# One ring of four PSUM banks for attention's transposes, products and mixing outputs, in place of two rings of two

## The chip, the cores and the metric

The kernel runs on one core of a Trainium2 chip. The metric is the device time of one execution in microseconds (us), lower is better; three runs of the kernel before gave 731.08, 732.12 and 732.07 us, median 732.07. The engines are named as the profile names them: PE is TensorE's matmul (PEld its weight load), DVE is VectorE, ACT is ScalarE, POOL is GpSimd, SP is SyncE, which issues the loads.

## What is computed

Causal attention over 2 batches, 12 heads, 448 positions and 64 channels per head, then two layers on the (2, 448, 768) result, all in float32:

```python
def _attn_ref(q, k, v):
    scores = scale * np.matmul(q, k.transpose(0, 1, 3, 2))
    scores = np.where(mask, -1000000000.0, scores)
    scores = scores - np.max(scores, axis=-1, keepdims=True)
    attn = np.exp(scores)
    attn = attn / (np.sum(attn, axis=-1, keepdims=True) + 1e-09)
    return np.matmul(attn, v).astype(np.float32)

def _moe_ref(x, w_tok1, w_tok2, w_ch1, w_ch2):
    xt = x.transpose(0, 2, 1)
    h = np.maximum(xt @ w_tok1, 0.0) @ w_tok2
    u = x + h.transpose(0, 2, 1)
    h2 = np.maximum(u @ w_ch1, 0.0) @ w_ch2
    return (u + h2).astype(np.float32)

def _moe2_ref(x, w_ch1, w_ch2):
    mixed = np.real(np.fft.fft(np.fft.fft(x, axis=1), axis=2)).astype(np.float32)
    u = x + mixed
    un = (u - mu) / np.sqrt(var + 1e-06)
    ch = np.maximum(un @ w_ch1, 0.0) @ w_ch2
    return (u + ch).astype(np.float32)
```

The weights of the MLPs arrive as float64.

## The kernel before

**Stages.** Attention with token mixing takes the first 170 us or so; the first channel MLP, the Fourier transform and the second channel MLP follow. Products of full precision are made of three passes over operands split in a high and a low part (kh and kl, qh and ql, wh and wl). Weights are fetched as 64-bit words (`fetch`, L73) and turned into such parts by `convert_steps` (L76 to L101): two instructions on ScalarE (L82, L99), four on VectorE (L84, L85, L89, L93), one on GpSimd (L100). Some of these conversions are put between the steps of attention by `weights` (L415).

**One pair of heads.** Attention goes through 12 pairs of heads. `prep` loads k and q and splits them (L196 to L206). `scores(n, g)` makes the scores of pair n in three groups g of row blocks: matmuls (L230, L243) into a tile b_s, row maxima on VectorE (L247), exponentials on ScalarE (L256) into the tile p in SBUF. `transposes(n, u)` for u = 0 to 4 turns four 112x112 blocks of p each into a PSUM tile (L269), which is copied to the tile pt, by ScalarE for u = 1 and 3 (L274), by VectorE for u = 0, 2 and 4 (L276). `pv` multiplies pt with v (L284) and ScalarE copies the result to ots (L289). `finish` transposes the head outputs back (L305), and VectorE scales them with the row sums into x (L307), splits them (L313), GpSimd makes the low part (L314).

**Token mixing.** After every third pair half a batch is complete. `mix_in` (L330, evicted by L336 on ScalarE and L337 on VectorE) and `channels_first` (L342, evicted by L345 on ScalarE) run in the steps `mix_first` and `mix_second`; three steps `mix_out` (L364, evicted by L366 on VectorE) follow. `next_mix` puts two such steps into each iteration.

**The order of the work.** TensorE's order is written out by hand (L424 on); the loop's n, by which the stages are named here, runs from 0 to 13. An iteration issues, in this order: scores(n, 0), pv of pair n - 2, scores(n, 1), transposes u = 0 and 1 of pair n - 1, a mixing step, transposes u = 2, scores(n, 2), transposes u = 3 and 4, a mixing step, finish of pair n - 2. The order on the other engines is the scheduler's, which also decides which free bank a new tile takes; every engine then works its queue off in order.

**PSUM.** It has eight banks, all used here: b_s has two buffers of two banks; tiles b_t (`transposes`, `channels_first`) share two banks; tiles b_y (`ybank`: pv, `finish`, `mix_in`, `mix_out`, and the last group of scores of the very first pair) share two others. The lines that say so:

```python
        ps = actx.enter_context(tc.tile_pool(name="aps", bufs=2, space=bass.MemoryType.PSUM))

        def ybank():
            return ps.tile([128, 512], F32, tag="y", name="b_y")
...
            tv = ps.tile([128, 512], F32, tag="t", name="b_t", bufs=2)
```

A tile that takes a bank waits until the bank's last content has been copied out. `spread` (L714), in the second MLP, has two small tiles r and nt.

Of the kernel before, what the change touches and what calls it, by code (L numbers as in the profile page):

```python
# [10 lines left out]
F32 = mybir.dt.float32  # L11
# [10 lines left out]
TS = 112  # L22
NI = S // TS
# [19 lines left out]
def fused_kernel(ctx: ExitStack, tc: tile.TileContext, qk, v, w1, w2, wa, wb, wc, wd, fa, fa0, fb, out):  # L43
# [107 lines left out]
    with ExitStack() as actx:  # L151
        ps = actx.enter_context(tc.tile_pool(name="aps", bufs=2, space=bass.MemoryType.PSUM))

        def ybank():
            return ps.tile([128, 512], F32, tag="y", name="b_y")

        ap = actx.enter_context(tc.tile_pool(name="attn", bufs=2))
        a1 = actx.enter_context(tc.tile_pool(name="attn1", bufs=1))
# [53 lines left out]
        def scores(n, g):  # L212
# [5 lines left out]
            if n or g < 2:  # L218
                sp = ps.tile([128, 2, 512], F32, tag="s", name="b_s", bufs=2)
                se = [sp[:TS, e] for e in range(2)]  # L220
            else:
                se = [ybank()[:TS] for e in range(2)]
# [38 lines left out]
        def transposes(n, u):  # L261
            c = pairs[n]
            if u == 0:
                c.pt = ap.tile([TS, 5, S], F32, tag="pt", name="pt", bufs=1)
            tv = ps.tile([128, 512], F32, tag="t", name="b_t", bufs=2)
            col = 0
            for e, j in (((0, 0),), ((1, 0),), ((0, 1), (0, 3)), ((1, 1), (1, 3)), ((0, 2), (1, 2)))[u]:
                for i in range(j, NI):
                    nc.tensor.transpose(  # L269
                        tv[:TS, col : col + TS], c.p[:, e, OFF[i] + j * TS : OFF[i] + (j + 1) * TS], ident[:TS, :TS]  # L270
                    )
                    col += TS
            if u in (1, 3):
                mark[1] = act.copy(c.pt[:, u], tv[:TS, :S]).ins  # L274
            else:
                mark[0] = vec.tensor_copy(c.pt[:, u], tv[:TS, :S]).ins  # L276

        def pv(n):
            c = pairs[n]
            c.ot = ybank()  # L280
            for j in range(NI):
                for e in range(2):
                    u, col = ((e, 0), (2 + e, 0), (4, 224 * e), (2 + e, 336))[j]
                    mm(  # L284
                        c.ot[D * e : D * e + D, j * TS : S], lhsT=c.v[:, j, D * e : D * e + D],
                        rhs=c.pt[:, u, col : col + TS * (NI - j)], start=j == 0, stop=j == NI - 1,
                    )
            c.ots = ap.tile([128, S], F32, tag="ots", name="ots")
            act.copy(c.ots, c.ot[:, :S])  # L289

        def finish(n):
            c = pairs[n]
            b, hf, pr = n // 6, n % 6 // 3, n % 3
            if pr == 0:
                h = Pair()
                halves[2 * b + hf] = h
                h.x = ap.tile([TS, NI, XW], F32, tag="x32", name="x32", bufs=1)
                h.h = ap.tile([TS, NI, XW], F32R, tag="xh", name="xh", bufs=1)
                h.l = ap.tile([TS, NI, XW], F32R, tag="xl", name="xl", bufs=1)
            h = halves[2 * b + hf]  # L300
            vec.tensor_scalar(out=c.ssum, in0=c.ssum, scalar1=1.0e-9, scalar2=None, op0=ALU.add)
            vec.reciprocal(out=c.ssum, in_=c.ssum)
            xp = ybank()
            for i in range(NI):
                nc.tensor.transpose(xp[:TS, i * 128 : (i + 1) * 128], c.ots[:, i * TS : (i + 1) * TS], ident)  # L305
            sl = slice(hf + pr * 128, hf + pr * 128 + 128)
            vec.tensor_tensor(  # L307
                out=h.x[:, :, sl].rearrange("p i (e d) -> p i e d", e=2),
                in0=xp[:TS, :].rearrange("p (i e d) -> p i e d", i=NI, e=2),
                in1=c.ssum.to_broadcast([TS, NI, 2, D]),  # L310
                op=ALU.mult,
            )
            vec.tensor_copy(h.h[:, :, sl], h.x[:, :, sl])  # L313
            pool.tensor_tensor(out=h.l[:, :, sl], in0=h.x[:, :, sl], in1=f(h.h)[:, :, sl], op=ALU.subtract)  # L314
            if hf and pr == 2:
                vec.tensor_copy(h.x[:, :, 0:1], h.x[:, :, 384:385])
                copied = vec.tensor_copy(h.h[:, :, 0:1], f(h.h)[:, :, 384:385])
                if n == 6 * B - 1:
                    hold.append(copied.ins)
                pool.tensor_copy(h.l[:, :, 0:1], f(h.l)[:, :, 384:385])  # L320
# [16 lines left out]
            vec.scalar_tensor_tensor(out=tl, in0=hp[:, :384], scalar=0.0, in1=f(th), op0=ALU.max, op1=ALU.subtract)  # L337

        def channels_first(n, pr):
            xt = ps.tile([128, 512], F32, tag="t", name="b_t", bufs=2)  # L340
            for i in range(NI):
                nc.tensor.transpose(  # L342
                    xt[:, i * TS : (i + 1) * TS], halves[n].x[:, i, pr * 128 : (pr + 1) * 128], ident[:TS, :TS]
                )
            act.copy(resid[3 * (n % 2) + pr][n // 2], xt[:, :S])  # L345

        def mix_first(n, t):
            mix_in(n, t)
            channels_first(n, 0)

        def mix_second(n, t):
            mix_in(n, t)
            channels_first(n, 1)
            channels_first(n, 2)
# [69 lines left out]
        with tc.manual_schedule(engines={mybir.EngineType.PE}):  # L424
            for n in range(np_ + 2):
# [15 lines left out]
                if old:  # L441
                    transposes(n - 1, 0)
                    transposes(n - 1, 1)
# [3 lines left out]
                if old:  # L447
                    transposes(n - 1, 2)
# [23 lines left out]
    ps = ctx.enter_context(tc.tile_pool(name="ps", bufs=1, space=bass.MemoryType.PSUM))  # L472
# [4 lines left out]
    def bank(tag=None):  # L477
        if tag is None:
            tag = cyc[turn[0] % 8]
            turn[0] += 1  # L480
        return ps.tile([128, 512], F32, tag=tag, name="b_" + tag, bufs=depth[tag])
# [232 lines left out]
    def spread(b, p):  # L714
        acc = rstd[b]
        var = bank()[:TS, :NI]
        with tc.issue_after(tail[0]):
            for i in range(NI):
                mm(var[:, i : i + 1], lhsT=acc[:, i * TS : (i + 1) * TS], rhs=mean_w[:, :1], start=True, stop=True)
        r = p.tile([TS, 16], F32, name=f"r{b}")[:, :NI]  # L720
        nt = p.tile([TS, 16], F32, tag="nt", name="nt")[:, :NI]
        act.activation(out=r, in_=var, func=AF.Sqrt, bias=eps_t[:TS], scale=1.0)
        vec.reciprocal(out=r, in_=r)
        vec.tensor_tensor(out=nt, in0=r, in1=r, op=ALU.mult)
        vec.scalar_tensor_tensor(out=nt, in0=var, scalar=EPS, in1=nt, op0=ALU.add, op1=ALU.mult)
        vec.tensor_scalar(out=nt, in0=nt, scalar1=-0.5, scalar2=1.5, op0=ALU.mult, op1=ALU.add)
        vec.tensor_tensor(out=r, in0=r, in1=nt, op=ALU.mult)
        inv[b] = r
# [34 lines left out]
    with tc.tile_pool(name="g2", bufs=1) as gpool, tc.tile_pool(name="tp", bufs=2) as tpool:  # L763
        wide_pool[0] = gpool
        late = {4: lambda: variance(0, gpool), 5: lambda: variance(1, gpool),
                6: lambda: spread(0, gpool), 7: lambda: spread(1, gpool)}
        for n in range(3):
            g = mlp_up(gpool, wc[n], 8, () if n else ahead, None if n else late)
            mlp_down(wd[n], g, scaled_store if n == 2 else scaled_add, 1)
# [73 lines left out]
```

## Time and profile before

| what | value |
|---|---|
| median of three runs | 732.07 us |
| the profiled execution's own time | 731.05 us |
| its span in the profile | 729.3 us |
| PE busy | 698.6 us, 96% of the span |
| PEld busy | 630.3 us, 86% |
| DVE busy | 523.6 us, 72% |
| ACT busy | 285.1 us, 39% |
| POOL busy | 275.3 us, 38% |
| chain of work that ended last | PE 77%, DVE 12%, ACT 5% of the span |

The profiled execution lies 1.0 us below the median. Busy shares are averages over stages with different limits. In a timeline the bracket at a line's end is the idle time of that engine just before the line, and what ended it; matmuls are pipelined, so that a line's duration reaches past the next line's start.

### The profile page before, as it was taken

Reading aid. Unit: us, or ns where it says so; the run is one execution under the profiler, and the core shown is the slowest. Engines: PE = TensorE matmul, PEld = TensorE weight load, DVE = VectorE, ACT = ScalarE, POOL = GpSimd, SP = SyncE. Lnnn points to the kernel's source line nnn. Section 1 sums busy time; section 2 is a strip of 40 time slices with the busy share of each in tenths; the row PEclk is TensorE's granted clock in tenths of the full one; section 3 lists DMA queues with packets and bytes.
Section 4 is the critical chain, followed back from the end, with each engine's and each line's share of the span. In section 5 each row is a group of like instructions: output and inputs, shape, how many; then the busy total and the mean of one; then the engine's idle time right before and its main releaser. Section 6 shows DMA issues by size and latency. Waiting matters only on the chain.

```text
span 729.3 us, 10268 instructions
## 1 busy us (share of the span) xinstructions
PE 698.6 (96%) x3940; PEld 630.3 (86%) x3940; DVE 523.6 (72%) x808; ACT 285.1 (39%) x600; POOL 275.3 (38%) x197
## 2 busy tenths in 40 slices
PE   6889899999999999999899999999999999999997
PEld 4668677878899999998689999999999999999996
DVE  5888887455698895688979997767945686945722
ACT  7777767334224333223353452223432222432200
POOL 3233634255133242241377334465323446321210
PEclk9989999999999999999999999999999999999999
DMA  8142411018533433210022242242321434322311
GB/s 265 54 127 88 140 35 56 30 32 263 138 137 118 148 125 115 87 44 0 1 86 87 88 146 102 100 173 90 131 97 58 145 106 155 114 89 83 113 50 51
DMA packets 20608, 74.15 MB, mean 102 GB/s; under 512 B 2364, under 2 KB 6974, under 8 KB 20192
## 3 DMA queue, kind: packets, MB, share of 16 engines
q1 hardware_dynamic: 19952, 69.48, 28.4%
q0 software_dynamic: 608, 4.03, 1.9%
q8 instruction: 31, 0.51, 0.3%
q14 instruction: 17, 0.14, 0.1%
HBM read 70.75 MB, written 2.75 MB: 101 GB/s over the span
## 4 chain that ended last, share of the span: by engine, by line
PE 77%; DVE 12%; ACT 5%; DMA 2%; POOL 2%; issue 2%; ACTq 0%; POOLq 0%; SPq 0%; DVEq 0%
PE b_s L144 6%; PE b_s L145 6%; PE b_s L143 6%; PE b_s L506 5%; PE b_s L507 5%; PE b_s L508 5%; PE b_t L508 3%; PE b_s L230 3%; PE b_t L506 3%; PE b_t L507 3%; PE b_t L143 2%; PE b_t L144 2%; PE b_t L145 2%; PE b_t L269 2%; ACT p L256 2%; PE b_y L284 2%
## 5 line engine op out<-in xcount | busy, mean ns | idle before, releaser
L100 POOL TENSOR_TENSOR wl<-m,wh 128x512 fp32r<-128x512 f32 (+1 forms) x90 | 149.4, 1660 | 253.6 <-ACT wh L99 240.9
L82 ACT ACTIVATE m<-w 128x512 f32<-128x512 f32 (+2 forms) x92 | 71.2, 773 | 165.9 <-POOL wl L100 131.7
L84 DVE TENSOR_SCALAR m<-m 128x512 f32<-128x512 f32 (+2 forms) x92 | 51.5, 560 | 88.8 <-ACT m L82 88.7
L89 DVE SCALAR_TENSOR_TENSOR m<-w,m 128x512 uint32<-128x512 uint32 (+2 forms) x92 | 101.2, 1101 | 2.4
L93 DVE SCALAR_TENSOR_TENSOR m<-w,m 128x512 uint32<-128x512 uint32 (+2 forms) x92 | 100.2, 1090 | 1.5
L99 ACT CAST wh<-m 128x512 fp32r<-128x512 f32 (+1 forms) x90 | 63.3, 703 | 94.3 <-DVE m L93 51.4
L143 PE MATMUL b_s<-acth,wh 128*128 128x448 f32 x240 | 87.2, 363 | 1.5 <-DVE resid L366 1.5
L144 PE MATMUL b_s<-acth,wl 128*128 128x448 f32 x240 | 86.9, 362 | 0.0
L145 PE MATMUL b_s<-actl,wh 128*128 128x448 f32 x240 | 86.6, 362 | 0.0
L506 PE MATMUL b_s<-gh,wh 128*128 128x448 f32 x208 | 75.7, 364 | 0.0
L508 PE MATMUL b_s<-gl,wh 128*128 128x448 f32 x208 | 75.3, 362 | 0.0
L507 PE MATMUL b_s<-gh,wl 128*128 128x448 f32 x208 | 75.2, 362 | 0.0
L256 ACT ACTIVATE p<-b_s,nmx 112x112 f32<-112x112 f32 (+3 forms) x94 | 45.3, 497 | 24.9 <-DVE nmx L247 20.6
L748 POOL TENSOR_TENSOR resid<-t,resid 128x448 f32<-128x448 f32 x24 | 33.7, 1402 | 49.5 <-DVE t L747 46.1
L85 DVE TENSOR_SCALAR m<-m 128x512 uint32<-128x512 uint32 (+2 forms) x92 | 49.6, 540 | 2.2
L143 PEld LDWEIGHTS b_s<-acth,wh 128*128 128x128 f32 x240 | 45.0, 187 | 4.8 <-issue 1.8
L145 PEld LDWEIGHTS b_s<-actl,wh 128*128 128x128 f32 x240 | 45.0, 187 | 3.1
L144 PEld LDWEIGHTS b_s<-acth,wl 128*128 128x128 f32 x240 | 45.0, 188 | 2.9
L508 PE MATMUL b_t<-gl,wh 128*128 128x448 f32 x120 | 43.6, 363 | 1.3 <-DVE gl L147 1.3
L506 PE MATMUL b_t<-gh,wh 128*128 128x448 f32 x120 | 43.7, 364 | 0.0
L507 PE MATMUL b_t<-gh,wl 128*128 128x448 f32 x120 | 43.4, 362 | 0.0
L269 PE MATMUL b_t<-ident,p 112*112 112x112 f32 x240 | 32.3, 274 | 11.5 <-DVE pt L276 6.4
(260 smaller groups left out, 1538.3 us busy)
## 6 DMA issues: line engine op xcount, KB each, us to landing
w<-in_wc SPq DMA_DIRECT2D x24, 768.0 KB, 4.3
w<-in_wd SPq DMA_DIRECT2D x36, 512.0 KB, 3.2
w<-in_wa SPq DMA_DIRECT2D x12, 768.0 KB, 4.2
w<-in_wb SPq DMA_DIRECT2D x18, 512.0 KB, 3.3
resid<-in_qk SPq DMA_DIRECT2D x24, 224.0 KB, 2.7
v<-in_v SPq DMA_DIRECT2D x12, 224.0 KB, 2.6
out<-t SPq DMA_DIRECT2D x12, 224.0 KB, 1.9
w<-in_w SPq DMA_DIRECT2D x2, 896.0 KB, 9.8
```

The lines of the kernel that those rows point to most:

```text
L82: act.activation(out=m, in_=hi.bitcast(F32), func=AF.Abs)
L89: vec.scalar_tensor_tensor(out=mu, in0=lo, scalar=29, in1=mu, op0=ALU.logical_shift_right, op1=ALU.bitwise_or)
L93: vec.scalar_tensor_tensor(out=mu, in0=hi, scalar=0xC0000000, in1=mu, op0=ALU.bitwise_and, op1=ALU.bitwise_or)
L99: act.copy(wh, m)
L100: pool.tensor_tensor(out=wl, in0=m, in1=f(wh), op=ALU.subtract)
L143: mm(pb[:, :S], lhsT=lh, rhs=act_h[ct][b], start=ct == 0, stop=False)
L144: mm(pb[:, :S], lhsT=ll, rhs=act_h[ct][b], start=False, stop=False)
L145: tail[0] = mm(pb[:, :S], lhsT=lh, rhs=act_l[ct][b], start=False, stop=ct == NCT - 1).ins
L256: mark[3] = act.activation(out=c.p[:, e, OFF[i] : OFF[i] + w], in_=se[e][:, c0 : c0 + w], func=AF.Exp, bias=c.nmx[:, i, e], scale=1.0, acc ...
L506: mm(pb[:, :S], lhsT=lh, rhs=gh, start=j + k == 0, stop=False)
L507: mm(pb[:, :S], lhsT=ll, rhs=gh, start=False, stop=False)
L508: tail[0] = mm(pb[:, :S], lhsT=lh, rhs=gl, start=False, stop=j == last and k == nk - 1).ins
```

## The change

All tiles of the tag "t" become tiles of the tag "y", and "y" gets four banks:

```diff
         def ybank():
-            return ps.tile([128, 512], F32, tag="y", name="b_y")
+            return ps.tile([128, 512], F32, tag="y", name="b_y", bufs=4)
@@ transposes
-            tv = ps.tile([128, 512], F32, tag="t", name="b_t", bufs=2)
+            tv = ybank()
@@ channels_first
-            xt = ps.tile([128, 512], F32, tag="t", name="b_t", bufs=2)
+            xt = ybank()
@@ spread
-        r = p.tile([TS, 16], F32, name=f"r{b}")[:, :NI]
-        nt = p.tile([TS, 16], F32, tag="nt", name="nt")[:, :NI]
+        r = p.tile([TS, 32], F32, name=f"r{b}")[:, :NI]
+        nt = p.tile([TS, 32], F32, tag="nt", name="nt")[:, :NI]
```

The number of PSUM banks in use stays eight. TensorE's instructions keep their order; what their first matmul waits for changes. On TensorE, n = 3, the first three transposes of pair 2 (the number in b_t and b_y is the tile's; in brackets the engine whose count of finished work is waited for), before:

```order
L269 MATMUL b_t_533<-ident_67,p_343 112x112 [waits PE_49]
L269 MATMUL b_t_533<-ident_67,p_343 112x112 x3
L269 MATMUL b_t_539<-ident_67,p_343 112x112 [waits PE_49]
L269 MATMUL b_t_539<-ident_67,p_343 112x112 x3
L269 MATMUL b_t_545<-ident_67,p_343 112x112 [waits Activation_49]
L269 MATMUL b_t_545<-ident_67,p_343 112x112 x3
```

and with the change:

```order
L269 MATMUL b_y_533<-ident_67,p_343 112x112 [waits PE_49]
L269 MATMUL b_y_533<-ident_67,p_343 112x112 x3
L269 MATMUL b_y_539<-ident_67,p_343 112x112 [waits PE_49]
L269 MATMUL b_y_539<-ident_67,p_343 112x112 x3
L269 MATMUL b_y_545<-ident_67,p_343 112x112 [waits DVE_49]
L269 MATMUL b_y_545<-ident_67,p_343 112x112 x3
```

The third tile took the bank of the second, 539, and waited for ScalarE's copy of it (L274); it now takes the bank that `finish` of pair 0 left, and waits for L307 of the iteration before. In n = 1, 2 and 4 the third tile changes in the same way: to the bank of the first pair's scores, to one that nobody reads any more, and to that of L307 of the iteration before.

On TensorE, n = 7, the last two transposes of pair 6 and the head transposes of pair 5, before:

```order
L269 MATMUL b_t_1149<-ident_67,p_893 112x112 [waits Activation_49]
L269 MATMUL b_t_1149<-ident_67,p_893 112x112 x3
L269 MATMUL b_t_1155<-ident_67,p_893 112x112 [waits DVE_49]
L269 MATMUL b_t_1155<-ident_67,p_893 112x112 x3
L305 MATMUL b_y_1163<-ident_67,ots_1084 112x128 x4
```

and with the change:

```order
L269 MATMUL b_y_1149<-ident_67,p_893 112x112 [waits DVE_49]
L269 MATMUL b_y_1149<-ident_67,p_893 112x112 x3
L269 MATMUL b_y_1155<-ident_67,p_893 112x112 [waits Activation_49]
L269 MATMUL b_y_1155<-ident_67,p_893 112x112 x3
L305 MATMUL b_y_1163<-ident_67,ots_1084 112x128 [waits DVE_49]
L305 MATMUL b_y_1163<-ident_67,ots_1084 112x128 x3
```

Tile 1149 (u = 3) waited for ScalarE's copy of u = 1 and now waits for VectorE's of u = 0; tile 1155 (u = 4) waited for VectorE's copy of u = 2 and now waits for ScalarE's of u = 1; the head transposes, which had a free bank, now wait for L366, the eviction of the mixing output just before. In n = 5 the fourth and fifth transposes come to stand behind ScalarE's copy of u = 1 and behind L345, and the second `mix_in` behind L337 of the first; in n = 8, L342 waits for VectorE's copy of u = 0 before and after, and the transposes behind it change from ScalarE's copy of u = 1 to an older ots copy (L289).

On VectorE, the scheduler moved the split of q (L204) in the first pairs. In n = 3, from the copies of pair 2's first transposes on, before:

```order
L276 COPY pt<-b_t 112x448 x2
L204 SCALAR_TENSOR_TENSOR ql<-resid_1_85,qh 128x448
L247 TENSOR_REDUCE nmx<-b_s 112x2
L276 COPY pt<-b_t 112x448
L307 TENSOR_TENSOR x_455<-b_y,ssum 112x4x128
L313 CAST xh<-x_455 112x4x128
```

and with the change:

```order
L276 COPY pt<-b_y 112x448 x2
L247 TENSOR_REDUCE nmx<-b_s 112x2
L276 COPY pt<-b_y 112x448
L307 TENSOR_TENSOR x_455<-b_y,ssum 112x4x128
L204 SCALAR_TENSOR_TENSOR ql<-resid_1_85,qh 128x448
L313 CAST xh<-x_455 112x4x128
```

L204 stands behind the maxima, the last pt copy and L307 now; the same move is made in n = 1 (behind the maxima and one copy) and n = 2. L301 and L302, two short instructions on the row sums, change places with neighbours at three places before n = 6. On ScalarE the casts of kh and qh (L198, L200) change places in n = 1 and n = 4, and on SP the loads of k and q (L196, L197) of two pairs. From n = 6 on all engines have the order of before. The wider r and nt move the tiles that lie behind them in the second MLP's pool by 128 or 192 bytes.

## Rows read from the trace of the kernel before

**Rows 1.** Windows: start:end, length, busy us of each engine, PEclk, DMA share, GB/s

```profile
137.00:729.00 592.00, 578.80 (x2912) 535.38 (x2911) 418.18 (x628) 188.60 (x316) 225.15 (x148) 1.00 0.30 102
...
20.00:120.00 100.00, 90.04 (x794) 70.87 (x792) 84.77 (x144) 73.24 (x215) 40.91 (x29) 0.96 0.29 89
...
0.00:20.00 20.00, 12.77 (x110) 10.43 (x112) 11.67 (x23) 14.31 (x43) 7.06 (x19) 0.91 0.80 242
...
40.00:60.00 20.00, 17.40 (x131) 14.29 (x130) 15.86 (x26) 15.14 (x42) 8.15 (x5) 0.83 0.41 133
...
100.00:120.00 20.00, 18.05 (x162) 14.50 (x160) 18.13 (x30) 14.89 (x44) 10.08 (x8) 0.95 0.16 50
```

**Rows 2.** Waits of PE, 0 to 200 us: us in total, times, longest

```profile
PE b_t L269 <- DVE pt L276: 6.4, 6, 2.2
PE b_t L269 <- ACT pt L274: 5.0, 5, 1.3
...
PE b_y L284 <- DVE resid L366: 0.7, 2, 0.4
...
PE b_t L342 <- DVE pt L276: 0.4, 1, 0.4
```

**Rows 3.** Timeline of PE, n = 1 to 5: start, length in us

```profile
14.66 0.60 PE L269 MATMUL b_t<-ident,p 112*112 112x112 f32 x4 [2.18 <-DVE pt L276]
...
24.33 0.59 PE L269 MATMUL b_t<-ident,p 112*112 112x112 f32 x4 [0.97 <-ACT pt L274]
...
42.02 0.60 PE L269 MATMUL b_t<-ident,p 112*112 112x112 f32 x4 [1.50 <-DVE pt L276]
...
45.01 1.74 PE L269 MATMUL b_t<-ident,p 112*112 112x112 f32 x8 [1.04 <-DVE pt L276]
...
57.30 0.98 PE L269 MATMUL b_t<-ident,p 112*112 112x112 f32 x8
```

**Rows 4.** Timeline of ACT: last exponential of scores(1, 0), and L345 in n = 5

```profile
14.12 0.27 ACT L256 ACTIVATION_READ_ACCUMULATOR p<-b_s,nmx 112x1 f32 x1
...
56.03 0.60 ACT L345 COPY resid<-b_t 128x448 f32<-128x448 f32 x1
```

**Rows 5.** Timeline of DVE, n = 2 to 5

```profile
26.17 0.63 DVE L204 SCALAR_TENSOR_TENSOR ql<-resid,qh 128x448 fp32r<-128x448 f32 x1 [0.36 <-ACT qh L200]
...
34.73 0.63 DVE L204 SCALAR_TENSOR_TENSOR ql<-resid,qh 128x448 fp32r<-128x448 f32 x1 [0.59 <-ACT qh L200]
...
46.79 0.62 DVE L276 COPY pt<-b_t 112x448 f32<-112x448 f32 x1 [0.30 <-PE b_t L269]
47.64 0.69 DVE L307 TENSOR_TENSOR x<-b_y,ssum 112x512 f32<-112x512 f32 x1 [0.23 <-PE b_y L305]
...
49.57 0.92 DVE L247 TENSOR_REDUCE nmx<-b_s 112x2 f32<-112x224 f32 x2 [0.29 <-PE b_s L243]
```

**Rows 6.** Timeline of PE, n = 7

```profile
79.90 0.60 PE L269 MATMUL b_t<-ident,p 112*112 112x112 f32 x4 [0.93 <-ACT pt L274]
81.18 0.59 PE L269 MATMUL b_t<-ident,p 112*112 112x112 f32 x4 [0.68 <-DVE pt L276]
81.61 0.60 PE L305 MATMUL b_y<-ident,ots 128*112 128x128 f32 x4
```

**Rows 7.** Timeline of ACT, n = 7: the copy of u = 1

```profile
79.28 0.56 ACT L274 COPY pt<-b_t 112x448 f32<-112x448 f32 x1
```

**Rows 8.** Timeline of DVE, n = 7 and n = 8

```profile
79.97 0.62 DVE L366 TENSOR_TENSOR resid<-b_y,resid 128x448 f32<-128x448 f32 x1
...
88.87 0.61 DVE L276 COPY pt<-b_t 112x448 f32<-112x448 f32 x1
```

**Rows 9.** Timeline of PE, n = 8

```profile
89.54 0.60 PE L342 MATMUL b_t<-ident,x 112*128 112x112 f32 x4 [0.41 <-DVE pt L276]
91.48 0.60 PE L269 MATMUL b_t<-ident,p 112*112 112x112 f32 x4 [1.34 <-ACT pt L274]
```

**Rows 10.** Instructions of line L147: duration in ns, min/median/max

```profile
L147 DVE SCALAR_TENSOR_TENSOR gl<-b_s,gh x40: 607/617/626, 141.2 to 667.2; 128x448 fp32r<-128x448 f32 x40
```

## The prediction

> **What bounds the kernel now.** I read the windows first: they say in which stage an engine can still be moved [rows 1]. From 137 us to the end TensorE (PE) is busy for 578.80 of 592 us at a granted clock of 1.00, and no instruction behind 170 us is moved, so a gain made in attention should pass through to the end undiminished. In the middle of attention, 20 to 120 us, TensorE is busy for 90.04 of 100 us and VectorE (DVE) for 84.77: TensorE sets the pace, VectorE is a close second. Three 20 us windows of attention have granted clocks of 0.91, 0.83 and 0.95. If the lower of the two levels (1.2 against 2.4 GHz) makes up the difference, 1.8, 3.4 and 1.0 us of full-speed work were lost there.
>
> Next, what TensorE waits for [rows 2]. Up to 200 us the matmuls that write tiles b_t and b_y stand still 12.5 us for their evictions: 6.4 + 5.0 + 0.4 + 0.7. Each means that a tile needs a bank whose last content is still being copied out. That is the whole stake, together with the clock that such pauses may cost.
>
> **The change, part by part.** No instruction is added or removed; TensorE's order is the same. What changes is which eviction a tile waits for, a few places on VectorE, ScalarE and SP in the first five pairs, and addresses. So I walk along the stalls and ask of each what is late next. Stages are named by the loop's n.
>
> *n = 1.* The third transposes stood 2.18 us until 14.66, for the eviction of the first [rows 3]. They now take a bank that the first pair's scores left long ago, so they start at 12.48. Behind them stands scores(1, 2), which needs the exponentials of scores(1, 0); those end at 14.12 + 0.27 = 14.39 [rows 4]. It began at about 14.66 + 0.60 = 15.26 and can begin at about 14.45: **0.8 us**, not 2.18. Bounds: 0 if the clock falls longer here, 2.18 + 1.8 if the low clock of this window goes too; I take the row's value.
>
> *n = 2 to 5.* Four more stalls go as such: 0.97, 0.94 in the same place of n = 3, 1.50 and 1.04 [rows 3], 4.45 us, and with them perhaps the 3.4 us of low clock behind the last two. TensorE can't keep that. VectorE's queue is nearly full here, and each pair ends with ScalarE working from VectorE's row maxima. Apart from one wait for a weight conversion, which stays, VectorE's idle time between 26 and 50 us is 0.36 and 0.59 us ahead of L204, waiting for qh, and 0.30, 0.23 and 0.29 us waiting for TensorE, which the stalls had made late [rows 5]. L204 now stands behind the maxima, a pt copy and L307, all of which are ready earlier, so the first two go, and the last three go with the stalls: 1.77 us. ScalarE's chain behind the maxima at 49.57 was unbroken up to L345 at 56.03 + 0.60 = 56.63 [rows 4]; it ends 1.8 us earlier. The fifth transposes of n = 5 now take L345's bank, and TensorE reaches them 0.4 us into the row at 57.30 [rows 3], 57.7 us, 1.0 us behind that eviction. So TensorE gains 1.8 + 1.0 = **2.8 us** and waits away the rest. Bounds: 1.0 if VectorE gains nothing, 4.45 + 3.4 = 7.9 if it never binds.
>
> *n = 7.* Two stalls, 0.93 and 0.68 us [rows 6]. The fourth transposes now wait for a copy of the stage's first, done long ago; the fifth wait for the second copy on ScalarE, which ends at 79.28 + 0.56 = 79.84 [rows 7], and the head transposes (L305) for L366 at 79.97 + 0.62 = 80.59 [rows 8] instead of starting at 81.61 [rows 6]. Both evictions come 2.8 us earlier like everything, so L305 gains a further 81.61 - 80.59 = **1.0 us**, with a new wait of about 0.6 us left in front of it. Bounds 0 and 1.61.
>
> *n = 8.* L342 waits for the same eviction as before, the copy at 88.87 [rows 8]; VectorE had no gap since 79.97, so it comes 2.8 us earlier and not 3.8, and the 0.41 us wait [rows 9] grows by 1.0. Behind it the 1.34 us wait [rows 9] goes, since that tile now waits for an ots copy that is older. Held by the next two evictions, TensorE leaves the stage where it entered: **0**. Bounds -1.0 and 1.75.
>
> *n = 9 to 13.* The wait of P times V on L366, 0.4 of the 0.7 us [rows 2], goes: **0.4 us** (0 to 0.4). n = 10 repeats n = 7, with 0.4 us less slack on VectorE: **0.6 us** (0 to 1.5). In n = 12 and 13 VectorE is half idle, so the other two short stalls go: **0.6 us** (0 to 0.6). The low clock around 118 us cost 1.0 us in its window [rows 1]; the stalls ahead of it shrink but don't vanish, so I count **0.7** (0 to 1.6, the upper end with what reaches the next window).
>
> *New waits.* Every tile of the ring now stands in TensorE's queue behind some eviction, and all later matmuls behind it: transposes behind the ots copy or L307, L305 behind pt copies, the second mix_in behind L337. Apart from those priced above the walk finds each of these done before TensorE arrives. ScalarE's swap of kh and qh and SP's swap of the two loads concern casts for a later pair. The wider r and nt move tiles of the second MLP by 128 or 192 bytes; L147 takes 607 to 626 ns wherever its tile lies [rows 10], so I count nothing, 0.5 us either way at most.
>
> Sum: 0.8 + 2.8 + 1.0 + 0 + 0.4 + 0.6 + 0.6 + 0.7 = 6.9 us. From the profiled execution's 731.05 us that gives 724.2; the median of the three runs, 732.07, is 1.0 us higher, and against it the forecast is **725.2 us**.
>
> **Rivals.** *VectorE holds it.* If L204's move doesn't close its gaps, and contention keeps VectorE's instructions where they are, only 0.8 + 1.0 + 0.4 + 0.6 = 2.8 us stay: 729.3 us. For it speak 84.77 busy us in 100; against it, that the gaps in [rows 5] were waits, not work. Chance 0.16.
>
> *Everything goes.* All 12.5 us of stalls, and some of the 6.2 us of lost clock: 9.5 us and more, 722.5 us down to 713.4. Against it stands the chain from maxima to exponentials, which no bank shortens. Chance 0.10.
>
> *Nothing changes.* The ring doesn't do what it says: each tile's new partner is as late as its old one, since all come from the same two in-order queues, as in n = 8. Then 732 us, within 0.2% (1.5 us, about what can be told from no change). Against it: the stalls of n = 2 to 4 wait for copies of the same pair, and the new partners are a pair older. Chance 0.07.
>
> *Slower, through the clock.* In 40 to 60 us the clock fell behind two stalls of 1.50 and 1.04 us and cost 3.4 us [rows 1, 3]. In the changed kernel TensorE arrives early at n = 4, 5 and 7 and waits there, in more and shorter pieces. If low clock follows each, in stages where TensorE and not VectorE is late, it must cost over 6.9 + 1.5 us to make the kernel slower, two and a half stretches like that one: 734 us or more. Against it, stalls of 0.97 and 1.34 us [rows 3, 9] were followed by a clock of 1.00. The Trainium skill speaks for this rival ("TensorE: Matmul & The Clock Gate", section "A second HAM failure mode: psum-queue depth-cycling"): a kernel that cycled through PSUM banks in every iteration left TensorE idle for moments between groups, and its clock went to and fro between the two levels. By that rule a ring of four would bring this rival, and not the forecast; the trace agrees only so far as its low stretches follow bank waits, and has bank waits without one. Chance 0.05.
>
> **How the numbers follow.** The forecast has the remaining 0.62. Faster by over 0.2%: 0.62 + 0.16 + 0.10 = 0.88; within it 0.07; slower 0.05. The range is 719.5 to 730.0 us: it takes in the forecast's open terms (the clock, VectorE's gaps), the first rival, and the nearer part of the second, and leaves out the last two (0.12) and some 0.08 of the far end and the tails.
>
> **What would show it.** Right: TensorE's waits on evictions in b_y tiles fall from 12.5 to some 3 to 5 us, what is left stands at n = 4 or 5, 7, 8 and 10, and new waits of score blocks on exponentials appear, 1.4 us in n = 1 first; VectorE's gaps ahead of L204 before 50 us are gone; the first MLP matmul behind 170 us (L143) starts some 7 us earlier and the rest of the trace is the old one, shifted. Wrong: a gain at 60 us of under 2 or over 5 us; a clock under 0.9 in a window behind 60 us; new waits on weights behind 190 us, which would mean that conversions don't come earlier with attention.

## The result, and the profile after

The changed kernel takes 724.46 us (median; 723.05 to 726.92), the kernel before beside it 732.10: ratio 0.9901, 95% interval 0.9874 to 0.9928. A second comparison gave 723.81 us, ratio 0.9904 (0.9874 to 0.9934). The forecast was 725.2 us, in a range of 719.5 to 730.0. The profiled execution of the changed kernel took 723.05 us, its span is 721.3, against 731.05 and 729.3.

The windows of the changed kernel that answer to [rows 1] (start:end, length, busy us of PE, PEld, DVE, ACT, POOL, then PEclk, DMA share, GB/s):

```profile
137.00:721.00 584.00, 570.56 (x2870) 528.35 (x2868) 415.42 (x623) 185.96 (x312) 223.02 (x147) 0.99 0.31 103
20.00:120.00 100.00, 92.31 (x828) 72.80 (x826) 86.11 (x145) 76.42 (x231) 41.90 (x29) 0.98 0.29 91
0.00:20.00 20.00, 13.13 (x134) 10.55 (x134) 12.69 (x26) 14.24 (x44) 7.04 (x19) 1.00 0.80 242
40.00:60.00 20.00, 18.04 (x146) 14.53 (x148) 17.15 (x29) 14.92 (x42) 8.29 (x6) 0.91 0.41 129
100.00:120.00 20.00, 18.47 (x167) 14.54 (x166) 16.65 (x29) 15.18 (x47) 10.07 (x7) 1.00 0.15 51
```

TensorE is busier by 2.3 us in the middle of attention and its clock there is up from 0.96 to 0.98; behind attention little has changed but the start (of the 8.24 us gained there 8.0 are left at the end). Where the 8 us were gained in these two executions, by the start of single instructions on TensorE's timeline:

| first matmul of | before, us | after, us | gain | forecast by then |
|---|---|---|---|---|
| n = 2 | 18.18 | 16.23 | 1.95 | 0.8 |
| n = 6 | 61.52 | 57.38 | 4.14 | 3.6 |
| n = 8 | 82.14 | 77.00 | 5.14 | 4.6 |
| n = 11 | 117.96 | 112.21 | 5.75 | 5.6 |
| L143 behind attention | 170.66 | 162.42 | 8.24 | 6.9 |

What TensorE waits for up to 200 us, to be laid beside [rows 2] (us in total, times, longest):

```profile
PE b_s L230 <- ACT p L256: 3.4, 4, 1.6
PE b_y L269 <- ACT ots L289: 3.4, 4, 1.5
...
PE b_y L305 <- DVE pt L276: 1.5, 1, 1.5
PE b_y L342 <- DVE pt L276: 1.3, 1, 1.3
...
PE b_y L269 <- ACT resid L345: 0.2, 1, 0.2
PE b_y L269 <- DVE pt L276: 0.2, 1, 0.2
```

The 12.5 us of waits for evictions are down to 3.4 + 1.5 + 1.3 + 0.2 + 0.2 = 6.6 us. In their place score blocks wait for exponentials of their bank (L230): 3.4 us, one of them at 9.67 us, where the trace before waits 0.59 us too. The places, from TensorE's timeline of the changed kernel (start, length, in brackets the idle time ahead and what ended it):

```profile
14.41 0.46 PE L230 MATMUL b_s<-kh,qh 64*112 64x448 f32 x2 [1.58 <-ACT p L256]
...
22.91 1.03 PE L269 MATMUL b_y<-ident,p 112*112 112x112 f32 x8 [0.47 <-ACT ots L289]
...
30.45 0.46 PE L230 MATMUL b_s<-kh,qh 64*112 64x448 f32 x2 [0.82 <-ACT p L256]
...
40.44 0.60 PE L269 MATMUL b_y<-ident,p 112*112 112x112 f32 x4 [0.53 <-ACT ots L289]
...
42.56 1.10 PE L305 MATMUL b_y<-ident,ots 128*112 128x128 f32 x4 [1.52 <-DVE pt L276]
...
74.19 0.60 PE L269 MATMUL b_y<-ident,p 112*112 112x112 f32 x4 [0.85 <-ACT ots L289]
...
85.31 0.60 PE L342 MATMUL b_y<-ident,x 112*128 112x112 f32 x4 [1.31 <-DVE pt L276]
...
109.41 0.59 PE L269 MATMUL b_y<-ident,p 112*112 112x112 f32 x4 [1.53 <-ACT ots L289]
```

The third transposes' stalls of n = 1 and 2 [rows 3] are gone, and the wait at 14.41 is the one that was forecast with 1.4 us (1.58 measured). Those at n = 2, 4, 7 and 10 on ScalarE's ots copy were not forecast. What holds TensorE at n = 4 shows in the chain of waits of the changed kernel (start, us, engine and what):

```profile
36.46 1.64 ACT p L256 x8
38.10 0.69 ACT w1h L99
...
38.92 1.06 ACT m L82
...
40.00 1.98 DVE m L84
41.97 0.54 DVE pt L276
...
42.56 1.10 PE b_y L305 x4
```

Exponentials, then two weight steps on ScalarE, a weight step on VectorE, a pt copy, and only then the head transposes. Back to 15 us hardly anything but ScalarE and VectorE stands in this chain.

### The profile page after: what moved, and what is told of

Read it like the earlier page. It is cut to its first block, busy times and chain, and to the rows that moved or that the text cites. A ratio compares the mean times of both kernels' runs of the same rounds, so it can differ in the third digit from the quotient of the medians.

```text
span 721.3 us, 10278 instructions
## 1 busy us (share of the span) xinstructions
PE 693.0 (96%) x3940; PEld 626.8 (87%) x3940; DVE 522.6 (72%) x808; ACT 283.6 (39%) x600; POOL 275.1 (38%) x197
## 4 chain that ended last, share of the span: by engine, by line
PE 77%; DVE 11%; ACT 4%; DMA 2%; POOL 2%; issue 2%; ACTq 0%; POOLq 0%; SPq 0%; DVEq 0%
PE b_s L145 6%; PE b_s L144 6%; PE b_s L143 6%; PE b_s L508 5%; PE b_s L507 5%; PE b_s L506 5%; PE b_t L508 3%; PE b_t L507 3%; PE b_t L506 3%; PE b_t L145 3%; PE b_t L144 2%; PE b_t L143 2%; PE b_y L284 2%; PE b_y L330 2%; DMA w<-in_wb 2%; PE b_s L230 2%
## 5 line engine op out<-in xcount | busy, mean ns | idle before, releaser
L100 POOL TENSOR_TENSOR wl<-m,wh 128x512 fp32r<-128x512 f32 (+1 forms) x90 | 149.1, 1657 | 254.3 <-ACT wh L99 241.3
L82 ACT ACTIVATE m<-w 128x512 f32<-128x512 f32 (+2 forms) x92 | 71.0, 773 | 168.6 <-POOL wl L100 126.5
L84 DVE TENSOR_SCALAR m<-m 128x512 f32<-128x512 f32 (+2 forms) x92 | 51.6, 561 | 91.9 <-ACT m L82 91.9
L89 DVE SCALAR_TENSOR_TENSOR m<-w,m 128x512 uint32<-128x512 uint32 (+2 forms) x92 | 101.8, 1108 | 2.4
L99 ACT CAST wh<-m 128x512 fp32r<-128x512 f32 (+1 forms) x90 | 63.3, 703 | 93.9 <-DVE m L93 53.3
L143 PE MATMUL b_s<-acth,wh 128*128 128x448 f32 x240 | 86.7, 361 | 1.6 <-DVE resid L366 1.6
L143 PEld LDWEIGHTS b_s<-acth,wh 128*128 128x128 f32 x240 | 44.9, 187 | 5.0 <-issue 1.9
L507 PEld LDWEIGHTS b_s<-gh,wl 128*128 128x128 f32 x208 | 39.1, 188 | 3.0
```

Of the source, the lines that this page charges most:

```text
L82: act.activation(out=m, in_=hi.bitcast(F32), func=AF.Abs)
L84: vec.tensor_scalar(out=m, in0=m, scalar1=F64_MIN, scalar2=F64_MAX, op0=ALU.max, op1=ALU.min)
L89: vec.scalar_tensor_tensor(out=mu, in0=lo, scalar=29, in1=mu, op0=ALU.logical_shift_right, op1=ALU.bitwise_or)
L99: act.copy(wh, m)
L100: pool.tensor_tensor(out=wl, in0=m, in1=f(wh), op=ALU.subtract)
L143: mm(pb[:, :S], lhsT=lh, rhs=act_h[ct][b], start=ct == 0, stop=False)
```

## Experiments

My theory: TensorE waited because a tile's bank had been left too recently; in a ring of four shared by all kinds its partner is older, until the chain over VectorE and ScalarE becomes the bound. Rivals: addresses; the order that the scheduler gave VectorE; the third bank for transposes alone, or sharing alone.

**Addresses.** Only r and nt of the kernel before made wider:

```diff
-        r = p.tile([TS, 16], F32, name=f"r{b}")[:, :NI]
+        r = p.tile([TS, 32], F32, name=f"r{b}")[:, :NI]
```

(nt likewise.)

> The kernel before with only the wider r and nt (32 instead of 16 columns); no instruction moves, some tiles of the second MLP lie 128 or 192 bytes higher. My theory (the gain of 8 us is made in attention by the ring of four banks): 732 us, ratio to the kernel before within 0.2%. The rival 'layout' (part of the gain comes from addresses): faster by 1 us or more.

731.39 us, ratio 0.9987 (0.9972 to 1.0003). At most 0.3% comes from here, by the interval's end.

**Order.** The kernel before with L204 of pairs 3 to 5 at its later places:

```diff
-                if n == 1:
-                    order.enter_context(tc.issue_after(mark[2]))
+                for ins in {1: mark[2:3], 3: mark[:1], 4: scaled, 5: scaled}.get(n, []):
+                    order.enter_context(tc.issue_after(ins))
```

(scaled holds the last L307.)

> The kernel before with its two rings of two banks, but L204 of the pairs 3, 4 and 5 held back on VectorE to the places that it has with the ring of four. My theory (banks): the stalls of TensorE on b_t and b_y tiles stay near 12.5 us, the time is 731 to 732.5 us, at best 1 us less for the closed gaps of VectorE (0.36 and 0.59 us). The rival 'order' (the scheduler's new order of VectorE is what helps): 728 us or less, at least half of the 8 us.

731.15 us, ratio 0.9992 (0.9973 to 1.0011). The waits in two rings stay as in [rows 2]:

```profile
PE b_t L269 <- DVE pt L276: 6.6, 6, 2.2
...
PE b_t L269 <- ACT pt L274: 4.0, 5, 1.1
```

So the order alone gives nothing that can be told from no change (by the interval at most 0.3%), and closing VectorE's gaps ahead of L204 [rows 5] gains nothing visible while the banks hold TensorE.

**A shared ring of three.** `bufs=3` in place of `bufs=4`.

> The changed kernel with a ring of three banks instead of four (seven PSUM banks in use). In an iteration without mixing the third transposes then wait for the ots copy instead of the copy of the first transposes, which is about as much room as before; with mixing the third transposes wait for the copy of the first as before, and the head transposes for a pt copy. If sharing is what helps, whatever the number of banks: within 2 us of the changed kernel, 724 to 726.5. If the number of tiles between a tile and its bank's last content decides (my theory): most of the gain goes in n = 5 to 11 and some stays in n = 1 to 4; 728 to 733 us.

736.91 us, ratio 1.0063 (1.0045 to 1.0081): slower than the kernel before, at 733 the expectation ended too low. Its waits:

```profile
PE b_y L330 <- DVE pt L276: 5.3, 2, 2.8
...
PE b_y L364 <- ACT ots L289: 4.5, 2, 2.4
```

The head transposes of n = 4 begin at 43.28 us, 3.3 us earlier than before; those of n = 9 at 109.74, 3.2 us later. As my theory has it, the gain is there without mixing, where a tile's partner is old, and turns round where mixing tiles come between. Some of the loss may be the clock: in 60 to 100 us it was 0.92 and 0.90 in this trace, and 1.00 before. Sharing alone is not what helps.

**Three and one.** Two rings, three banks for transposes, one for everything else:

```diff
-            return ps.tile([128, 512], F32, tag="y", name="b_y")
+            return ps.tile([128, 512], F32, tag="y", name="b_y", bufs=1)
...
-            tv = ps.tile([128, 512], F32, tag="t", name="b_t", bufs=2)
+            tv = ps.tile([128, 512], F32, tag="t", name="b_t", bufs=3)
```

> Two rings again, but three banks for transposes and channels_first and one for P times V, mixing outputs and head transposes (the last group of scores of the very first pair takes two of the three). The rival 'a third bank for the transposes is all that was needed': 723 to 727 us. My theory (what helps is that the tiles of all kinds take turns): the waits on transposes go, but every b_y tile now waits for the tile just before it (mixing outputs for the ots copy, head transposes for L337 or L366), so new waits of some 0.6 us in each of eleven iterations: 729 us or more, perhaps slower than the kernel before.

745.87 us, ratio 1.0187 (1.0165 to 1.0209). The transposes' waits fall to 3.6 us, and the tiles with one bank pay:

```profile
PE b_y L305 <- DVE resid L366: 4.3, 3, 1.9
PE b_y L284 <- DVE x L307: 4.2, 4, 1.5
PE b_y L364 <- ACT ots L289: 3.4, 3, 1.4
PE b_y L330 <- ACT ots L289: 3.3, 2, 2.3
PE b_y L364 <- DVE resid L366: 2.8, 2, 1.7
```

Of the divisions that were run only four banks with all kinds in turn gain. One bank for the transposes and three for the rest was not run.

The next runs ask what bounds the changed kernel. The first three of them ran beside it, on one chip; the later four ran on two other chips, and are compared with it by their ratios to the kernel before on the same chip. The changed kernel:

> The changed kernel itself, beside the next three on the same chip: 724 to 725 us, ratio to the kernel before 0.990.

723.81 us, as above.

**A pt copy for ScalarE.** `if u in (0, 1, 3)` in place of `if u in (1, 3)`.

> The changed kernel, with the copy of the first transposes (u = 0) made by ScalarE instead of VectorE, 12 copies of 0.55 to 0.62 us. My theory (after the change VectorE, busy 86 of 100 us, and the chain maxima, exponentials behind it hold TensorE in n = 2 to 8): the waits of TensorE on VectorE's pt copies and on exponentials shrink, 721 to 724 us. The rival (ScalarE's queue is what comes last: exponentials, and the ots copies, which already cost 3.4 us of waits): the copy of u = 1 and the ots copy come later, waits on ScalarE grow by more than those on VectorE shrink, 726 us or more.

727.13 us, ratio 0.9939 (0.9915 to 0.9962), 3.3 us slower than the changed kernel. The rival holds: its transposes now wait 2.8 us for copies L274 in two places, 1.9 us the longest, and the head transposes 0.5 us, where none waited for them. ScalarE has no room either.

**Two weight steps later.**

```diff
-        parts = [0, 0, 1, 1] + 7 * [2] + [1, 1, 0]
+        parts = [0, 0, 1, 1, 2, 2, 1, 1] + 5 * [2] + [0]
```

> The changed kernel with two steps of the weight conversion moved from n = 6 and 7, where VectorE is busy 18.2 of 20 us, to n = 11 and 12, where it is busy about half the time. If VectorE's load in n = 6 to 8 holds TensorE there: the waits at n = 7 and 8 (0.85 us on the ots copy, 1.3 us of L342 on VectorE's copy of u = 0) shrink, 0.5 to 1.5 us faster than the changed kernel. If they are set by something else: same time. A miss would be a new wait of the early matmuls on weights in n = 12 and 13, then slower.

722.98 us, ratio 0.9888 (0.9859 to 0.9917), 0.8 us less than the changed kernel. The wait of 0.85 us at n = 7 is gone, that of L342 on the copy of u = 0 is 0.44 us. This run's trace also has, by luck, the low clock at 15 to 20 us that the kernel before had (0.91 in 0 to 20 us). On its timeline, P times V of n = 2 and the head transposes of n = 2 to 4:

```profile
18.71 2.25 PE L284 MATMUL b_y<-pt,v 112*64 112x448 f32 x16
...
24.64 0.60 PE L305 MATMUL b_y<-ident,ots 128*112 128x128 f32 x4
...
32.27 0.60 PE L305 MATMUL b_y<-ident,ots 128*112 128x128 f32 x4
...
42.67 0.88 PE L305 MATMUL b_y<-ident,ots 128*112 128x128 f32 x4 [1.53 <-DVE pt L276]
```

The changed kernel has them at 17.32, 23.77, 32.16 and 42.56 us: a delay of 1.4 us on TensorE is down to 0.1 at n = 3. TensorE has that much slack behind VectorE and ScalarE there.

**The ots copy first.** In the loop the weight steps come behind pv, and wait for its copy:

```diff
+                if n >= 2:
+                    pv(n - 2)
                 if live:
                     for _ in range(parts[n]):
-                        weights(mark[2:])
-                if n >= 2:
-                    pv(n - 2)
+                        weights(mark[2:] + ([pairs[n - 2].copied] if n >= 2 else []))
```

(copied is L289's instruction.)

> The changed kernel, with the weight steps of an iteration put behind the ots copy (L289) on ScalarE, 0.6 us of copy ahead of 0.6 to 0.9 us of L82 or L99. It takes away the four waits of transposes on the ots copy (0.47, 0.53, 0.85 and 1.53 us). If they are lost time: 721 to 722 us, 2.5 to 3.4 us faster than the changed kernel. My theory (in n = 2 to 5 VectorE holds the pace anyway, and L84 behind L82 comes 0.6 us later): the 2.4 us of n = 7 and 10 shrink to a part, 722.5 to 724 us.

724.23 us, ratio 0.9908 (0.9878 to 0.9938): nothing gained, less than either expectation. Its timeline of TensorE:

```profile
41.45 0.37 PE L230 MATMUL b_s<-kh,qh 64*112 64x256 f32 x2 [1.03 <-ACT p L256]
...
44.59 0.79 PE L284 MATMUL b_y<-pt,v 112*64 112x224 f32 x8 [0.53 <-DVE pt L276]
...
50.79 0.59 PE L269 MATMUL b_y<-ident,p 112*112 112x112 f32 x4 [1.12 <-DVE pt L276]
...
76.51 0.65 PE L305 MATMUL b_y<-ident,ots 128*112 128x128 f32 x4 [0.58 <-DVE resid L366]
```

All waits on the ots copy in front of transposes are gone, others stand a few instructions further on, and the head transposes of n = 7 begin at 76.51 against 76.44 us. The 3.4 us were only the place where TensorE waited for the two other engines. The window from 40 to 60 us has clock 1.00 here and 0.91 in the changed kernel, and 76.5 us is reached all the same. But clock and edit differ together, so that this run does not tell what the low clock cost in the changed kernel, where the chain of waits lies on TensorE alone from 42.56 to 70.5 us.

**Casts for GpSimd.** `(vec if pr == 2 else pool).tensor_copy(...)` in L313.

> The changed kernel, with the cast L313 (0.42 us on VectorE) of the first two of every three pairs made by GpSimd, 8 of 12; it lies in VectorE's queue right ahead of the row maxima of the next pair. My theory (VectorE's queue sets the pace of n = 2 to 8, since a start that came 1.4 us later in one run was made up by 32 us): the maxima of n = 4 and 5 come up to 0.8 us earlier and the kernel gains 0.5 to 1.5 us, 722.4 to 723.4 us. The rival (VectorE has slack, only single evictions count): no change against the 723.9 us of the changed kernel.

723.78 us, ratio 0.9888 (0.9865 to 0.9911), and 723.81 for the changed kernel on another chip: the gain that I expected does not show, though the ratios (0.9901 and 0.9904 for the changed kernel) are too wide to rule out 1 us. VectorE was not relieved in n = 2 and 3. Its timeline, and below it GpSimd's:

```profile
28.27 2.16 DVE L89 SCALAR_TENSOR_TENSOR m<-w,m 112x1024 uint32<-112x1024 uint32 x1
```

```profile
27.06 0.94 POOL L313 CAST xh<-x 112x512 fp32r<-112x512 f32 x1 [0.36 <-DVE x L307]
28.07 1.28 POOL L314 TENSOR_TENSOR xl<-x,xh 112x512 fp32r<-112x512 f32 x1
```

L89 takes 2.16 us instead of 1.69, because L314 moved under it: what the cast freed (0.42 us) went there. So this run does not speak against my theory, nor for it.

**Weight steps later still.** `parts = [0, 0, 1, 1, 2, 2, 1, 1, 1, 2, 1, 3, 3, 0]`.

> The changed kernel with three steps of the weight conversion moved from n = 6, 7 and 8 (and one from n = 10) to n = 11 and 12. The run with two steps moved gained about 0.9 us and left waits of 0.4 and 0.7 us at n = 8. If VectorE's and ScalarE's load there is the cause: 721.5 to 723 us. A miss: the early matmuls of the first MLP wait for weights behind 125 us, 724 us or more.

722.37 us, ratio 0.9861 (0.9838 to 0.9883), within the expectation, and 1.4 us below the casts' run on the same chip; no wait on weights appears behind 125 us.

**Three edits together.**

> The changed kernel with three edits together: casts L313 of two pairs in three on GpSimd, weight steps of n = 6 to 8 and 10 moved to n = 11 and 12, and the weight steps of an iteration behind the ots copy on ScalarE. By my theory, with VectorE relieved, the waits on the ots copy are lost time at last: 720.5 to 722.5 us. If ScalarE's chain from maxima to exponentials holds the pace whatever VectorE has left to do: 722.5 to 724 us.

722.22 us, ratio 0.9864 (0.9840 to 0.9888): the weight steps' gain (722.37 us on the same chip), and nothing from the other two edits.

**One weight step from n = 4 to n = 5.** `parts = [0, 0, 1, 1, 1, 3, 1, 1, 1, 2, 1, 3, 3, 0]`, which takes L84 out of the chain shown above.

> The run with weight steps moved to n = 11 and 12, and one more step (L84 and L85 of w2) moved from n = 4 to n = 5. In the changed kernel the chain of waits reaches the head transposes of n = 4 (L305 at 42.56 us) through L82, L84 (1.98 us on VectorE) and a pt copy. My theory (from 22 us on this chain over VectorE and ScalarE, not a bank as such, holds TensorE): the wait of L305 of 1.5 us goes and L305 of n = 4 comes 1 to 2 us earlier, about 41 us; n = 5 has 2.8 us of idle VectorE to take the step up; 720.5 to 722 us. The rival (TensorE is held by bank waits that another eviction takes over at once, as with the ots copy put first): L305 comes earlier but the scores or P times V behind it wait instead, the head transposes of n = 5 come at 57 us as before, 722 to 723.5 us.

721.36 us (721.08 to 722.13), ratio 0.9860 (0.9832 to 0.9889): the lowest median, 1.0 us below the weight steps later still, but on another chip, and by their ratios the two are alike (0.9860 and 0.9861). So the times show no gain from this step. On TensorE's timeline:

```profile
40.85 0.60 PE L305 MATMUL b_y<-ident,ots 128*112 128x128 f32 x4
...
49.82 0.60 PE L342 MATMUL b_y<-ident,x 112*128 112x112 f32 x4 [1.36 <-ACT ots L289]
...
52.95 0.60 PE L269 MATMUL b_y<-ident,p 112*112 112x112 f32 x4 [0.66 <-ACT resid L345]
```

L305 comes 2.0 us earlier than with the weight steps later still (42.89), without a wait. n = 5 takes one back, in waits further on, for the ots copy and L345, much as the rival foresaw (head transposes at 56.35 against 57.35; with the ots copy first they stood at 56.32). The other stays in the trace (n = 13: 144.11 against 145.04), but the clock in 40 to 60 us was 1.00 here and 0.91 there, 1.8 us of full-speed work, so it may be the clock's. Whether this step gains stays open. What the runs do show is that weight steps taken out of n = 6 to 8 move the time (0.8 us on one chip, 1.4 us on the other), and that rearranging who waits for a bank, as with the ots copy, does not.

## Why the prediction was right

**n = 1: 0.8 us, right.** scores(1, 2) begins at 14.41 instead of 15.18, 0.77 us, held by exponentials as forecast. By n = 2 a further 1.18 us have come, since the low clock of 0 to 20 us is gone (0.91 to 1.00). The forecast left this out of its sum. In the kernel before it is lost time: the run with only r and nt widened has a clock of 1.00 there, and its first matmuls of n = 2 and of L143, at 18.18 and 170.66 us in the kernel before, are

```profile
16.98 0.38 PE L230 MATMUL b_s<-kh,qh 64*112 64x256 f32 x2
...
169.34 0.44 PE L143 MATMUL b_s<-acth,wh 128*128 128x448 f32 x1 [1.51 <-DVE resid L366]
```

So 1.2 of the 8.24 us are a low clock that the kernel before does not have in every execution. With the ring of four it is slack: the run with two weight steps moved has it and is 0.1 us late at n = 3.

**n = 2 to 5: 2.8 us, measured 2.2.** The argument was right, that VectorE, and not TensorE's stalls (4.45 us), sets what can be gained. The gaps ahead of L204 closed:

```profile
26.87 0.61 DVE L204 SCALAR_TENSOR_TENSOR ql<-resid,qh 128x448 fp32r<-128x448 f32 x1
...
34.41 0.70 DVE L204 SCALAR_TENSOR_TENSOR ql<-resid,qh 128x448 fp32r<-128x448 f32 x1
...
40.00 1.98 DVE L84 TENSOR_SCALAR m<-m 128x896 f32<-128x896 f32 x1 [0.74 <-ACT m L82]
```

By the first matmul of n = 5 (43.59 us instead of 47.54) 2.0 us are there, for which the forecast had 1.8; of its 1.0 us ahead of L345 only 0.2 came. What failed is the place: TensorE does not run ahead until L345 in n = 5. It is held at n = 4 already, behind L82 and L84, by 1.52 us. How much of the 2.2 us is the clock (0.83 in 40 to 60 us before, 0.91 after) is open.

**n = 7: 1.0; n = 8: 0. Both as measured** (1.0 and 0.1). At n = 8 L342 waits 1.31 us, the forecast 0.41 + 1.0 = 1.41, and the 1.34 us behind it [rows 9] are gone. At n = 7 the wait stands ahead of the third transposes, on the ots copy, instead of ahead of L305.

**pv and n = 10: 0.4 + 0.6, measured 0.5** between n = 9 (91.92 us instead of 97.14) and n = 11. TensorE waits 1.53 us for the ots copy at n = 10, where the forecast saw no wait but its repeat of n = 7.

**Low clock around 118 us: 0.7, measured 1.6.** This is the term that was mis-sized most. The window from 115 to 125 us, before:

```profile
115.00:125.00 10.00, 8.60 (x67) 6.33 (x68) 7.92 (x15) 6.41 (x21) 2.40 (x2) 0.83 0.07 24
```

and after:

```profile
115.00:125.00 10.00, 10.00 (x88) 9.15 (x83) 6.74 (x13) 7.32 (x24) 1.05 (x1) 1.00 0.08 25
```

A clock of 0.83 was a loss of 0.17 x 10 = 1.7 us; the forecast saw an upper end of 1.6 and took less than half of it because the stalls ahead would not vanish. They did not (1.53 us), and the clock stayed up. Nor is it shown that the ring kept it up: the kernel before with only L204 moved has its two stalls there (0.86 and 0.70 us) and no low clock in this window:

```profile
115.00:125.00 10.00, 9.31 (x84) 7.65 (x86) 7.52 (x15) 7.05 (x23) 2.42 (x2) 1.00 0.08 24
```

n = 12 and 13 then gave 0.9 for the forecast 0.6.

**What was luck.** Without its clock term the forecast adds up to 6.2 us. Without the two low stretches, 1.2 + 1.6 us, the measured sum is 0.8 + 2.2 + 1.0 + 0.1 + 0.5 + 0.9 = 5.5 us. So the waits were worth somewhat less than forecast and the clock of these two executions 2.8 us instead of 0.7; that the total came so near is in part luck.

**Waits left: 3 to 5 us forecast, 6.6 found.** The walk took every ots copy for done, and overlooked the weight steps L82 and L99 that stand ahead of it on ScalarE. It cost the sum little: where the waits on the ots copy were taken away, the time did not fall (724.23 against 723.81 us).

**Rivals.** "VectorE holds it" (729.3) was too hard: the gaps closed, and 2.0 us came by n = 5 where the forecast had 1.8. "Everything goes" failed on the chain from maxima to exponentials, as argued. "Nothing changes" failed since the partners are older; in the ring of three, from n = 5 on, they are not. "Slower, through the clock": the Trainium skill's rule ("TensorE: Matmul & The Clock Gate", section "A second HAM failure mode: psum-queue depth-cycling") did not show as a cost here; the ring of four has the higher clock, 0.992 against 0.987, though its low stretch behind 42.56 us does follow a bank wait, of 1.52 us. (The forecast's own reading of such a stretch was loose: in the kernel before the matmuls were slow from 42.84 us on, behind the stall of 1.50 us alone, and the one of 1.04 us came later.)

That difference in clock is worth more than the 0.7 us of the sum. Over 55 runs of the kernel before the mean clock is 0.9870 and the mean time 731.89 us; over eight of the changed kernel 0.9916 and 724.43. Among the 55, the 11 at 0.984 average 733.59 us and the four at 0.990 average 730.07; a line through all falls by 5.1 us per 0.01. By it 0.0046 x 510 = 2.4 of the 7.5 us go with the clock (an estimate), over three times the forecast, and near the 2.8 us of the two traces. Whether fewer waits raise the clock, or which, no run settles: the run with only r and nt widened kept its waits and had clock 1.00 in 0 to 20 us.

## What to carry to other kernels

Read from the schedule which eviction each PSUM tile waits for and how long ago that was issued: rings of two that are filled in bursts can wait while the banks beside them lie free, and one shared ring can help if it is long enough for the burst (here four banks gained 7 to 8 us, and three lost 5). Then ask what is late next, and price a gain by that chain and not by the sum of the waits. An experiment that only moves a wait tells more than the wait's size: if the time stays, the wait was slack. And look at the clock of both traces before crediting a change with the difference of two executions: 2.8 of 8.2 us were the clock's here.

## What was not expected of the hardware

VectorE all but stood still while GpSimd worked, in some instructions. GpSimd's timeline in the changed kernel:

```profile
27.90 1.28 POOL L314 TENSOR_TENSOR xl<-x,xh 112x512 fp32r<-112x512 f32 x1 [1.42 <-DVE xh L313]
...
39.11 2.38 POOL L100 TENSOR_TENSOR w1l<-m,w1h 112x1024 fp32r<-112x1024 f32 x1 [2.30 <-ACT w1h L99]
```

L89 at 28.57 us (1.69 us long) overlaps L314 by 0.61 us, in the run with casts on GpSimd (2.16 us) by 1.08: in both 1.08 us are left outside the overlap. L84 at 40.00 overlaps L100 by 1.49 of its 1.98 us; moved to n = 5, away from L100, the same step takes 0.62 us:

```profile
46.72 0.62 DVE L84 TENSOR_SCALAR m<-m 128x896 f32<-128x896 f32 x1
```

So up to 1.4 of the 2.0 us won at n = 4 are GpSimd's subtraction no longer in the way. The Trainium skill says so ("Perfetto Trace Analysis", section "Optimizing Scalar/DVE Operations"): VectorE and GpSimd share a read port of SBUF, so that moving work from one to the other may not help. The casts' run agrees: L89 grew by 0.47 us there, the cast had taken 0.42.
